# Gated mix of a long convolution and an MLP: the middle of the convolution in groups of four j

## The chip, the cores and the metric

The kernel runs on one core of one Trainium2 chip. Its engines are TensorE (PE, with its weight loads listed as PEld), VectorE (DVE), ScalarE (ACT), GpSimd (POOL) and SyncE (SP), which issues most DMA transfers. The metric is the time of one execution on the device, in microseconds, as the median of several runs; lower is better.

## What is computed

```python
def _A_ref(q, k, v, shift_k, ssm_k, ssm_D):
    ...
    for t in range(ks):
        k_shift = k_shift + k_pad[:, t:t + S, :] * shift_k[:, ks - 1 - t][None, None, :]
    kv = k_shift * v
    L = 2 * S
    kv_pad = jnp.pad(kv, ((0, 0), (0, S), (0, 0)))
    kf_pad = jnp.pad(ssm_k, ((0, 0), (0, S)))
    ...
    y_f = kv_f * kf_f[None, :, :, :]
    y = (lambda x, s, axes=(-2,-1): jnp.fft.irfft2(x, s=s, axes=axes))(y_f, (1, L), axes=(1, 2))[:, 0, :S, :]
    y = y + kv * ssm_D[None, None, :]
    return q * y

def _B_ref(x, w1, w2):
    h = jnp.einsum("bsd,df->bsf", x, w1)
    zero = jnp.zeros_like(h)
    h = jnp.maximum(h, zero)
    return jnp.einsum("bsf,fd->bsd", h, w2)

g = _sigmoid((x * gate_w).sum(-1, keepdims=True))
return g * a + (1 - g) * b
```

The sequence has S = 2048 positions and D = 512 channels; the hidden width of the MLP is 1792. `a` is a causal convolution of 2048 taps for each channel, done by a Fourier transform of length 4096, `b` is an MLP of two matrix products, and both are float32.

## The kernel before, in words

**The MLP** is cut into four chunks of 512 positions and 14 slices of 128 hidden units. `mlp1(c, f)` (lines 305 to 307) makes one slice of the hidden layer in a PSUM bank, with twelve matmuls of 128x128 weights and 512 columns: each float32 operand is split into a high and a low part, and three products stand for one. ACT (L317, `hh`) applies the maximum and DVE (L320, `hl`) makes the low part, after which the bank is free. `mlp2(c, f)` (L332 to L334) adds the slice to four output banks `m2`, again with twelve such matmuls. In this text they are called full matmuls.

**The convolution** is a transform in two stages, 64 by 32 points, as matrix products. In the first stage (`stage1`, L371) float32 matmuls with 64 rows and 128 columns turn two inputs, the filter ("h") and the product of the shifted k and v ("x"), into 64 complex frequencies; ACT copies each bank to `ev` (L376), and SP stores it to the DRAM array `sa`. A matmul that uses only a part of PE's 128x128 array is a *tile* here: tiles in different rows or columns of the array can run together. Two tiles of 64x128 fill the array once, and one filling is called a *round*.

In the middle (`conv_mid(j)`, L453 to L501, for 32 values of j) a load `r` brings both inputs of j; tiles of 64 rows and 32 columns (L476) apply the second stage, eight tiles for one j, into a bank `fh` for the filter and `fx` for the signal. Each bank holds real parts in its lower and imaginary parts in its upper 64 partitions. ACT copies the filter's halves (L486 to L488, so that both orders of real and imaginary are at hand), DVE forms the complex product (`y`, `hb`, `ha`: L491, L492, L494, L495), ACT and DVE split it into high and low (`yh` L496, `yl` L497), and three full matmuls with constants `ci` from POOL's queue apply the first inverse stage (`three`, L446 to L448). ACT copies the bank to `bv` (L500), and SP stores it to the DRAM array `sb`. At the end (`conv_end`, L551) two positions n at a time go through the last inverse stage with tiles of 128 rows and 64 columns (`y`), and DVE forms the gated output.

**Order.** The program is written out by a planner (`Plan`). Every operation has a rank, a supposed duration, the operations that it depends on, and the buffers that it takes and gives back; at each moment the planner lets each engine take the ready operation of lowest rank. Convolution work on PE has ranks that start with 0, MLP work ranks that start with 1, so that the MLP fills PE between the pieces of the convolution. `SAFE` is an extra margin before an operation counts as ready. The result is one fixed order for each engine, with semaphores between them.

**PSUM** has eight banks here: four `m2` outputs, and four `cv` banks that `mlp1`, `stage1`, the middle and the end share.

Of the kernel before, what the change touches and what calls it, by code (L numbers as in the profile page):

```python
# [39 lines left out]
def _constants():  # L40
# [5 lines left out]
    s1 = np.stack([s1, s1.reshape(P, NJ, 2, 2)[:, :, ::-1].reshape(P, P)], 1)  # L46


    fw = np.zeros((NJ, 2, 2, 32, 2, 2, 32))
    iv = np.zeros((NJ, 2, 2, 32, 32, 2, 2))  # L50
    n2, k2 = np.arange(32)[:, None], np.arange(32)[None]
    kc = np.arange(32)[:, None]
    for j in range(NJ):
        for b in range(2):
            k1 = 2 * j + b
            c = _w((4 * k1 + 1 + 256 * k2) * n2)
            fw[j, b, 0, :, 0, b] = c.real
            fw[j, b, 1, :, 0, b] = -c.imag
            fw[j, b, 0, :, 1, b] = c.imag
            fw[j, b, 1, :, 1, b] = c.real  # L60
            c = np.conj(_w((4 * k1 + 1 + 256 * kc) * n2.T))
            iv[j, 0, b, :, :, b, 0] = c.real
            iv[j, 1, b, :, :, b, 0] = -c.imag
            iv[j, 0, b, :, :, b, 1] = c.imag
            iv[j, 1, b, :, :, b, 1] = c.real

    cf = np.stack([fw[:, b, :, :, :, b] for b in range(2)], 1)
    cf = np.stack([cf, cf[:, ::-1]], -3).reshape(NJ, P, P).transpose(1, 0, 2)
    ih, il = _split(iv.reshape(NJ, P, P))
    ci = np.ascontiguousarray(np.stack([ih, il], 1).transpose(2, 0, 1, 3))  # L70
# [4 lines left out]
    return s1, cf, ci, ib  # L75
# [7 lines left out]
class Plan:  # L83
# [6 lines left out]
    def add(self, eng, dur, rank, fn, deps=(), take=(), give=(), dma=0, fifo=()):  # L90
        rank = tuple(_flat(rank))
        op = dict(eng=eng, dur=dur, rank=rank, fn=fn, take=tuple(take), give=tuple(give), dma=dma, fifo=tuple(fifo),
# [10 lines left out]
    def order(self):  # L103
# [4 lines left out]
        out = []  # L108
# [9 lines left out]
        while True:  # L118
            for eng, ops in ready.items():
                if busy.get(eng, 0.0) > now + 1e-9:  # L120
                    continue
                best = None
                for op in ops:
# [4 lines left out]
                    if any(self.turn[q][0] != op["n"] for q in op["fifo"]):  # L128
                        continue
# [27 lines left out]
            while events and events[0][0] <= now + 1e-9:  # L157
                _, _, what, op = heapq.heappop(events)
                if what == "go":
                    ready.setdefault(op["eng"], []).append(op)  # L160
                    continue
# [3 lines left out]
                for o in op["next"]:  # L165
# [4 lines left out]
                    if not o["wait"]:  # L170
# [19 lines left out]
MM = 0.227  # L190
# [5 lines left out]
def build(tc, wf, xp, qn, kn, vn, hn, dn, sh, gw, w1, w2, cs1, ccf, cci, cib, out):  # L196
# [12 lines left out]
    sb = dram.tile([32, P, D], F32, name="sb")  # L209
    bd = dram.tile([16, P, D], F32, name="bd")  # L210

    room = {"raw": RAW, "x": XB, "cv": 4, "hh": 2, "m20": 1, "m21": 1, "m22": 1, "m23": 1, "o": OB, "in": IN, 
            "cf": 2, "acc": ACC, "tmp": TMP, "ev": EV, "r": RB, "ci": CIB, "ha": HAB, "y": YB, "yh": YHB, "bv": BVB,
# [99 lines left out]
    def mlp1_out(c, f, prev):  # L313
        i = c * NF + f

        def relu():
            nc.scalar.activation(tile_of(("hh", c, f), "hh", dt=F32R, p=mp, bufs=2), T["m1", c, f], AF.Relu)  # L317

        def rest():
            nc.vector.scalar_tensor_tensor(tile_of(("hl", c, f), "hl", dt=F32R, p=mp, bufs=2), T["m1", c, f], 0.0,  # L320
# [5 lines left out]
    def mlp2(c, f):  # L326
        i = c * NF + f
        for s in range(4):
# [7 lines left out]
            m2[c, s] = add("PE", 3 * MM, (1, i + 1.5, s), go, [hdone[c, f], wdone[1, f], m2.get((c, s))],  # L336
# [28 lines left out]
    def stage1(t, c, key, rank, after, give):  # L365
        for r in range(R):
            def go(r=r):
                z = slice(r * D, (r + 1) * D)
                for half in range(2):
                    at = slice(64 * half, 64 * half + 64)  # L370
                    mm(bank(("s1" + t, c, half, r)), T["s1t",][at, P * "hx".index(t):P * "hx".index(t) + P], T[key][at, z], start=True, stop=True)  # L371

            m = add("PE", SWITCH + TILES, (0, rank), go, [after, s1ld], ["cv", "cv"], give if r == R - 1 else ())
# [69 lines left out]
    def three(key, h, l, i, z):  # L443
        ps = bank(key)
        c = T["ci", key[1]][:, 2 * P * i:2 * P * (i + 1)]
        mm(ps, c[:, :P], T[h][:, z], start=True, stop=False)  # L446
        mm(ps, c[:, :P], T[l][:, z], start=False, stop=False)  # L447
        mm(ps, c[:, P:], T[h][:, z], start=False, stop=True)  # L448
# [250 lines left out]
```

## Time and profile before

| what | value |
|---|---|
| median of 3 runs | 439.27 us (438.4 to 439.63) |
| the profiled execution | 439.54 us |
| its span, first to last instruction | 437.8 us |
| mean granted clock of TensorE | 0.997 |
| moved by DMA | 98.35 MB, mean 225 GB/s |

A page of the profile lists busy time by engine, the chain of work that ended last, and groups of equal instructions with the mean length of one and the idle time before them. Rows in order of time have start, length, engine, line, operation, output and inputs, shape of weights, shape of operands and count. A float32 matmul appears as two passes, so that 256 tiles of the middle stand as 512 rows. Since matmuls are pipelined, the length of one is more than the distance to the next.

### The profile page before, as it was taken

Reading aid. Unit: us, or ns where it says so; the run is one execution under the profiler, and the core shown is the slowest. Engines: PE = TensorE matmul, PEld = TensorE weight load, DVE = VectorE, ACT = ScalarE, POOL = GpSimd, SP = SyncE. Lnnn points to the kernel's source line nnn. Section 1 sums busy time; section 2 is a strip of 40 time slices with the busy share of each in tenths; the row PEclk is TensorE's granted clock in tenths of the full one; section 3 lists DMA queues with packets and bytes.
Section 4 is the critical chain, followed back from the end, with each engine's and each line's share of the span. In section 5 each row is a group of like instructions: output and inputs, shape, how many; then the busy total and the mean of one; then the engine's idle time right before and its main releaser. Section 6 shows DMA issues by size and latency. Waiting matters only on the chain.

```text
span 437.8 us, 6154 instructions
## 1 busy us (share of the span) xinstructions
PE 428.2 (98%) x2157; PEld 288.4 (66%) x2157; DVE 286.0 (65%) x426; ACT 195.0 (45%) x355; POOL 18.3 (4%) x38
## 2 busy tenths in 40 slices
PE   8999999999999999999999999999999999999994
PEld 6575665675856675665665565567877777758883
DVE  4699999869574119778887989878047654631113
ACT  4535445436344316767777778766123211101110
POOL 0000000000000010100100010100000000000000
PEclk9999999999999999999999999999999999999998
DMA  8988897897969395867689688731477888800002
GB/s 270 339 316 277 296 298 277 277 308 272 298 212 362 132 301 150 244 203 253 195 290 297 203 264 254 230 120 52 146 290 251 322 322 271 290 7 0 1 0 96
DMA packets 51616, 98.35 MB, mean 225 GB/s; under 512 B 5073, under 2 KB 9937, under 8 KB 51458
## 3 DMA queue, kind: packets, MB, share of 16 engines
q1 hardware_dynamic: 46898, 93.61, 63.4%
q0 software_dynamic: 4688, 4.36, 4.5%
q8 instruction: 17, 0.28, 0.3%
q14 instruction: 13, 0.11, 0.1%
HBM read 65.44 MB, written 32.51 MB: 224 GB/s over the span
## 4 chain that ended last, share of the span: by engine, by line
PE 92%; DVE 3%; DMA 2%; ACT 1%; issue 0%; DVEq 0%; SPq 0%; ACTq 0%
PE m L332 13%; PE m L305 12%; PE m L334 11%; PE m L333 11%; PE m L307 11%; PE m L306 11%; PE fh L476 6%; PE s1h L371 4%; PE s1x L371 4%; PE y L551 3%; PE iv L446 2%; PE iv L447 2%; PE iv L448 1%; DMA raw<-w 1%; DMA ev<-wf 1%; DVE hl L320 1%
## 5 line engine op out<-in xcount | busy, mean ns | idle before, releaser
L332 PE MATMUL m<-w1h_h,hh 128*128 128x512 f32 x224 | 91.2, 407 | 0.9 <-ACT hh L317 0.9
L320 DVE SCALAR_TENSOR_TENSOR hl<-m,hh 128x512 fp32r<-128x512 f32 x56 | 38.5, 689 | 76.8 <-ACT hh L317 76.5
L334 PE MATMUL m<-w1h_h,hl 128*128 128x512 f32 x224 | 87.6, 391 | 0.1
L333 PE MATMUL m<-w1l_l,hh 128*128 128x512 f32 x224 | 87.4, 390 | 0.0
L317 ACT ACTIVATE hh<-m 128x512 fp32r<-128x512 f32 x56 | 33.4, 598 | 118.3 <-PE m L307 113.8
L305 PE MATMUL m<-xh_h,w0h_h 128*128 128x512 f32 x192 | 77.8, 405 | 0.0
L307 PE MATMUL m<-xh_h,w0l_l 128*128 128x512 f32 x192 | 75.0, 391 | 0.0
L306 PE MATMUL m<-xl_l,w0h_h 128*128 128x512 f32 x192 | 74.9, 390 | 0.0
L332 PEld LDWEIGHTS m<-w1h_h,hh 128*128 128x128 f32 x224 | 42.0, 187 | 34.8 <-issue 25.5
L305 PEld LDWEIGHTS m<-xh_h,w0h_h 128*128 128x128 f32 x192 | 36.0, 187 | 26.6 <-issue 14.7
L334 PEld LDWEIGHTS m<-w1h_h,hl 128*128 128x128 f32 x224 | 42.0, 188 | 9.8 <-DVE hl L320 0.5
L333 PEld LDWEIGHTS m<-w1l_l,hh 128*128 128x128 f32 x224 | 42.1, 188 | 7.7
L307 PEld LDWEIGHTS m<-xh_h,w0l_l 128*128 128x128 f32 x192 | 36.0, 188 | 8.0
L306 PEld LDWEIGHTS m<-xl_l,w0h_h 128*128 128x128 f32 x192 | 36.1, 188 | 6.7
L476 PE MATMUL fx<-r,cf 64*32 64x512 f32 x256 | 34.0, 601 | 0.0
L476 PE MATMUL fh<-r,cf 64*32 64x512 f32 x256 | 33.8, 601 | 0.0
L491 DVE TENSOR_TENSOR y<-fx,ha 128x512 f32<-128x512 f32 x32 | 22.1, 690 | 12.5 <-ACT ha L487 11.2
L428 DVE TENSOR_TENSOR acc<-acc,tmp 128x1024 f32<-128x1024 f32 x24 | 29.3, 1222 | 0.6
L486 ACT COPY ha<-fh 64x512 f32<-64x512 f32 x32 | 18.5, 579 | 23.5 <-PE fx L476 13.6
L464 POOL DMA_DIRECT2D ci<-cci x32 | 16.9, 529 | 274.1 <-DMA sa<-ev 152.3
L497 DVE TENSOR_TENSOR yl<-ha,yh 128x512 fp32r<-128x512 f32 x32 | 22.0, 689 | 5.1 <-ACT yh L496 4.8
L376 ACT COPY ev<-s1x 128x512 f32<-128x512 f32 x32 | 17.1, 595 | 17.7 <-PE s1x L371 14.0
(67 smaller groups left out, 514.2 us busy)
## 6 DMA issues: line engine op xcount, KB each, us to landing
sa<-ev SPq DMA_DIRECT2D x64, 256.0 KB, 2.7
r<-sa SPq DMA_DIRECT2D x32, 512.0 KB, 4.6
sb<-bv SPq DMA_DIRECT2D x32, 256.0 KB, 3.3
br<-sb SPq DMA_DIRECT2D x16, 512.0 KB, 4.8
raw<-w SPq DMA_DIRECT2D x26, 256.0 KB, 4.6
in<-kn SPq DMA_DIRECT2D x10, 512.0 KB, 5.4
raw<-xp SPq DMA_DIRECT2D x16, 256.0 KB, 4.6
in<-hn SPq DMA_DIRECT2D x8, 512.0 KB, 5.5
```

The lines of the kernel that those rows point to most:

```text
L305: mm(ps, part("h", f, k), T["x", "h", c, k], start=k == 0, stop=False)
L306: mm(ps, part("h", f, k), T["x", "l", c, k], start=False, stop=False)
L307: mm(ps, part("l", f, k), T["x", "h", c, k], start=False, stop=k == 3)
L317: nc.scalar.activation(tile_of(("hh", c, f), "hh", dt=F32R, p=mp, bufs=2), T["m1", c, f], AF.Relu)
L320: nc.vector.scalar_tensor_tensor(tile_of(("hl", c, f), "hl", dt=F32R, p=mp, bufs=2), T["m1", c, f], 0.0, T["hh", c, f].bitcast(F32), op0=O ...
L332: mm(ps, T["hh", c, f][:, z], T["w", "h", 1, f], start=f == 0, stop=False)
L333: mm(ps, T["hh", c, f][:, z], T["w", "l", 1, f], start=False, stop=False)
L334: mm(ps, T["hl", c, f][:, z], T["w", "h", 1, f], start=False, stop=f == NF - 1)
L371: mm(bank(("s1" + t, c, half, r)), T["s1t",][at, P * "hx".index(t):P * "hx".index(t) + P], T[key][at, z], start=True, stop=True)
L428: nc.vector.tensor_tensor(T["acc", c], T["acc", c], T[dst], op=OP.add)
L476: mm(ps[to:to + 32, :], cf[at, co:co + 32], r[at, z], start=True, stop=True)
L491: y = add("DVE", d, rank, lambda: tt(tile_of(k("y"), "y"), T[k("fx")], T[k("ha")], op=OP.mult), [fx, q2], ["y"], fifo=["y"])
```

## The change

**First stage.** The two pairs of tiles of one call are now one operation that takes four banks and needs one entry into tiles, where two operations of two banks were ordered by themselves. The constant table is half as large.

**Middle.** `conv_mid(g)` does four j at a time, for eight g. The forward tiles keep their 64x32 shape, but each round now writes, for one of real (o = 0) or imaginary (o = 1), the four j of one parity b to a bank of its own: two rounds for the filter, each an operation by itself, two for the signal in one or two pieces as the planner puts them. Real and imaginary parts so lie on the same partitions of different banks. ACT and DVE copy the filter's four banks to `ha`; DVE multiplies the signal's banks with them (eight products) and adds in four steps to `p`, which stays in float32 and isn't split. The first inverse stage is then sixteen float32 tiles of 32 rows and 64 columns, one row strip for each j and one bank for each j, in two rounds that add up. ACT and DVE copy two banks each to `bv`. Loads of `r` are one for each j and input; the constants of forward and inverse come together in `cc` on SP's queue, and POOL's loads of `ci` are gone. `sb` has another layout.

**Planner.** An operation says whether it is in tiles, and entering tiles is charged only once for neighbours. While ready work of rank 1 needs no bank, other rank 1 work may not take banks that a waiting tile operation needs. `SAFE` for PE goes from 2.1 to 1.0, there are three buffers `hh` for two, and `mlp2` is ranked one slice later.

```diff
-        for r in range(R):
-            def go(r=r):
+        def go():
+            for r in range(R):
                 z = slice(r * D, (r + 1) * D)
...
-            m = add("PE", SWITCH + TILES, (0, rank), go, [after, s1ld], ["cv", "cv"], give if r == R - 1 else ())
+        m = add("PE", R * TILES, (0, rank), go, [after, s1ld], ["cv"] * 2 * R, give, tiles=True)
...
+        def rounds(t, os):
+            for o in os:
+                ps = [bank(k("f", t, o, b)) for b in range(2)]
+                for j in range(4):
+                    for b in range(2):
+                        at = slice(64 * b, 64 * b + 64)
+                        mm(ps[b][32 * j:32 * j + 32, :], T[k("cc")][at, 64 * j + 32 * o:64 * j + 32 * o + 32],
+                           T[k("r", t, j // 2)][at, (j % 2) * D:(j % 2 + 1) * D], start=True, stop=True)
...
+                    def mul(o=o, b=b, i=i):
+                        src = T[k("ha", i ^ o, b)]
+                        tt(src if o else tile_of(k("p", i, b), "p"), T[k("f", "x", o, b)], src, op=OP.mult)
...
+                        def join(b=b, i=i):
+                            tt(T[k("p", i, b)], T[k("p", i, b)], T[k("ha", 1 - i, b)], op=OP.add if i else OP.subtract)
...
-        iv = add("PE", 3 * MM, (0, rank), lambda: three(k("iv"), k("yh"), k("yl"), 0, first), [yl, ci], ["cv"], ["yh", "ci"])
+        def inverse():
+            ps = [bank(k("iv", j)) for j in range(4)]
+            for o in range(2):
+                for b in range(2):
+                    for j in range(4):
+                        at = slice(32 * j, 32 * j + 32)
+                        c = 2 * P + P * o + 64 * b
+                        mm(ps[j][64 * b:64 * b + 64, :], T[k("cc")][at, c:c + 64], T[k("p", o, b)][at, :], start=o == 0, stop=o == 1)
+
+        iv = add("PE", 2 * TILES, (0, rank), inverse, list(y.values()), ["cv"] * 4, ["p"] * 4 + ["cc"], tiles=True)
...
-sb[n::16].rearrange("h p d -> p h d")
+sb[:, n::16]
...
-SAFE = dict(PE0=2.1, PE1=0.175, ACT=0, DVE=0.4)
+SAFE = dict(PE0=1.0, PE1=0.175, ACT=0, DVE=0.4)
...
+HHB = 3
+M2R = 2.5
```

Three places show what moves. On PE, in the first stage of the convolution before (`s1x` is the signal's tiles, L332 to L334 one part of `mlp2`):

```order
L371 MATMUL s1x_0_0_529<-acc_375,s1c_s1t 128x512
L371 MATMUL s1x_1_0_531<-acc_375,s1c_s1t 128x512
L332 MATMUL m_0_1_210<-w1h_h_5_392,hh_5_459 128x512
...
L371 MATMUL s1x_0_1_546<-acc_375,s1c_s1t 128x512
L371 MATMUL s1x_1_1_548<-acc_375,s1c_s1t 128x512
```

and there now (`s1h` is the filter, L341 to L343 `mlp2`, L314 the next `mlp1`, which takes a bank):

```order
L380 MATMUL s1x_0_0_394<-acc_284,s1c_s1t 128x512
L380 MATMUL s1x_1_0_396<-acc_284,s1c_s1t 128x512
L380 MATMUL s1x_0_1_398<-acc_284,s1c_s1t 128x512
L380 MATMUL s1x_1_1_400<-acc_284,s1c_s1t 128x512
L341 MATMUL m_0_0_202<-w1h_h_4_266,hh_4_350 128x512
...
L343 MATMUL m_0_3_244<-w1h_h_4_266,hl_4_367 128x512
L380 MATMUL s1h_0_0_444<-in_343,s1c_s1t 128x512
L380 MATMUL s1h_1_0_446<-in_343,s1c_s1t 128x512
L380 MATMUL s1h_0_1_448<-in_343,s1c_s1t 128x512
L380 MATMUL s1h_1_1_450<-in_343,s1c_s1t 128x512
L314 MATMUL m_0_5_465<-xh_h_0_102,w0h_h_5_369 128x512
```

The four tiles of one call now stand together, with twelve full matmuls to the next four.

On PE, in the middle before (`fh` and `fx` are the forward tiles of one j, `iv` the inverse of an earlier j):

```order
L334 MATMUL m_1_3_1158<-w1h_h_9_673,hl_9_1668 128x512
L476 MATMUL fh_1798<-r_1613,cf_1473 32x512 x4
L476 MATMUL fx_1799<-r_1613,cf_1473 32x512 x4
L446 MATMUL iv_1809<-yh_1766,ci_1638 128x512
L447 MATMUL iv_1809<-yl_1777,ci_1638 128x512
L448 MATMUL iv_1809<-yh_1766,ci_1638 128x512
L305 MATMUL m_1_11_1821<-xh_h_0_976,w0h_h_11_800 128x512
```

and now (`iv_1` is the inverse of group 1 with a bank for each j, `f_x` the signal of group 2):

```order
L343 MATMUL m_1_3_1160<-w1h_h_12_790,hl_12_1855 128x512
L524 MATMUL iv_1_1899<-p_0_1_1763,cc_1534 64x512
L524 MATMUL iv_1_1900<-p_0_1_1763,cc_1534 64x512
L524 MATMUL iv_1_1901<-p_0_1_1763,cc_1534 64x512
L524 MATMUL iv_1_1902<-p_0_1_1763,cc_1534 64x512
...
L524 MATMUL iv_1_1902<-p_1_1_1784,cc_1534 64x512
L341 MATMUL m_1_0_1087<-w1h_h_13_912,hh_13_1874 128x512
...
L343 MATMUL m_1_1_1097<-w1h_h_13_912,hl_13_1890 128x512
L476 MATMUL f_x_0_2_1941<-r_x_2_1768,cc_1726 32x512
...
L476 MATMUL f_x_1_2_1956<-r_x_2_1781,cc_1726 32x512
```

The inverse is sixteen tiles in a block, six full matmuls stand behind it, and then both rounds of the next signal follow in one block.

On DVE, in the middle now, for one group (products L506, copies L493, sums L513, an MLP slice L329):

```order
L506 TENSOR_TENSOR p_0_3_2159<-f_x_0_3_2137,ha_0_3_2032 128x512
...
L506 TENSOR_TENSOR ha_1_3_2034<-f_x_1_3_2150,ha_1_3_2034 128x512
L493 COPY ha_0_4_2205<-f_h_0_4_2186 128x512
L513 TENSOR_TENSOR p_0_3_2159<-p_0_3_2159,ha_0_3_2058 128x512
L513 TENSOR_TENSOR p_0_3_2167<-p_0_3_2167,ha_0_3_2032 128x512
L513 TENSOR_TENSOR p_1_3_2172<-p_1_3_2172,ha_1_3_2060 128x512
L493 COPY ha_0_4_2232<-f_h_0_4_2209 128x512
L513 TENSOR_TENSOR p_1_3_2180<-p_1_3_2180,ha_1_3_2034 128x512
L329 SCALAR_TENSOR_TENSOR hl_3_2255<-m_2_3_2221,hh_3_2249 128x512
```

Copies of the next group's filter now stand on DVE among the sums that the inverse waits for; before, all of the filter's copies were on ACT.

More of the change, by code (lines that the diff above doesn't have):

```diff
@@ L56, in _constants @@
             c = _w((4 * k1 + 1 + 256 * k2) * n2)
[L57 to L70, printed above, removed]
+            fw[b, 0, :, j, 0] = c.real
+            fw[b, 1, :, j, 0] = -c.imag
+            fw[b, 0, :, j, 1] = c.imag
+            fw[b, 1, :, j, 1] = c.real
+            c = np.conj(c.T)
+            iv[j % 4, :, j // 4, 0, b, 0] = c.real
+            iv[j % 4, :, j // 4, 1, b, 0] = -c.imag
+            iv[j % 4, :, j // 4, 0, b, 1] = c.imag
+            iv[j % 4, :, j // 4, 1, b, 1] = c.real
+    cc = np.concatenate([fw.reshape(P, 8, 2 * P), iv.reshape(P, 8, 2 * P)], 2)
     c = np.conj(_w((4 * np.arange(64)[:, None] + 1) * 32 * np.arange(64)[None])) / S
     ib = np.stack([c.real, -c.imag], 1).reshape(P, 64)
-    return s1, cf, ci, ib
+    return s1, cc, ib
 def _flat(r):
@@ L88, in __init__, with add @@
         self.room, self.ops, self.turn = dict(room), [], {}
[L90 removed]
+    def add(self, eng, dur, rank, fn, deps=(), take=(), give=(), dma=0, fifo=(), tiles=False):
         rank = tuple(_flat(rank))
[L92 removed]
+        op = dict(tiles=tiles, eng=eng, dur=dur, rank=rank, fn=fn, take=tuple(take), give=tuple(give), dma=dma, fifo=tuple(fifo),
                   wait=0, next=[], n=len(self.ops))
@@ L107, in order @@
         pipe = 0.0
-        out = []
+        out, soon, mode = [], [], False
         for op in self.ops:
@@ L122, in order @@
                 best = None
+                held = ()
+                if eng == "PE" and any(o["rank"][0] == 1 and not o["take"] for o in ops):
+                    held = {t for o in ops + soon if o["rank"][0] == 0 and len(o["take"]) > 1 for t in o["take"]}
                 for op in ops:
@@ L128, in order @@
                     if any(self.turn[q][0] != op["n"] for q in op["fifo"]):
+                        continue
+                    if op["rank"][0] and any(t in held for t in op["take"]):
                         continue
@@ L143, in order @@
                 free = now + op["dur"]
+                if eng == "PE":
+                    if op["tiles"] and not mode:
+                        free += SWITCH
+                    mode = op["tiles"]
                 if eng == "PE" and now < PE_COLD:
@@ L193, with build @@
 ROW = P * D * 4
-def build(tc, wf, xp, qn, kn, vn, hn, dn, sh, gw, w1, w2, cs1, ccf, cci, cib, out):
+def build(tc, wf, xp, qn, kn, vn, hn, dn, sh, gw, w1, w2, cs1, ccc, cib, out):
     nc = tc.nc
@@ L370, in go @@
                     at = slice(64 * half, 64 * half + 64)
-                    mm(bank(("s1" + t, c, half, r)), T["s1t",][at, P * "hx".index(t):P * "hx".index(t) + P], T[key][at, z], start=True, stop=True)
-            m = add("PE", SWITCH + TILES, (0, rank), go, [after, s1ld], ["cv", "cv"], give if r == R - 1 else ())
+                    mm(bank(("s1" + t, c, half, r)), T["s1t",][at, :], T[key][at, z], start=True, stop=True)
+        m = add("PE", R * TILES, (0, rank), go, [after, s1ld], ["cv"] * 2 * R, give, tiles=True)
+        for r in range(R):
             for half in range(2):
@@ L605, in build @@
     p2 = add("SP", 0.0, -1e3, lambda: phase(2), stores)
-    for j in range(NJ):
-        conv_mid(j, p2)
+    for g in range(NJ // 4):
+        conv_mid(g, p2)
     p3 = add("SP", 0.0, -1e3, lambda: phase(3), sbstores)
@@ L646 @@
 RB = 4
-CIB = 4
-HAB = 2
-YB = 1
-YHB = 2
-BVB = 2
+HS = 1
+XS = 1
+HD = 1
+VD = 1
+HHB = 3
+M2R = 2.5
+HAB = 8
+PB = 4
+BVB = 4
 BRB = 4
```

128 lines of the change are left out of this document (65 added, 63 removed).

## The prediction

> **What bounds the kernel now.** I read the page's busy shares first, then the chain that ended last, then PE's own waits, then PE's rows in order of time.
>
> ```profile
> PE 428.2 (98%) x2157; PEld 288.4 (66%) x2157; DVE 286.0 (65%) x426; ACT 195.0 (45%) x355; POOL 18.3 (4%) x38
> PE 92%; DVE 3%; DMA 2%; ACT 1%; issue 0%; DVEq 0%; SPq 0%; ACTq 0%
> 160.00:300.00 140.00, 139.09 (x948) 84.94 (x947) 116.24 (x173) 100.33 (x176) 14.78 (x28) 1.00 0.72 222
> PE iv L446 <- DVE hl L320: 0.9, 1, 0.9
> ```
>
> The first two rows are totals and chain: PE is busy 98% of the span and is 92% of the chain. The third is the stretch from 160 to 300 us, where the middle of the convolution runs between MLP matmuls (columns: length, busy PE, PEld, DVE, ACT, POOL, clock, DMA share, GB/s): PE is full at clock 1.00, DVE 83%, ACT 72%. The fourth is the only wait of PE in that stretch, 0.9 us. So the time is PE's work added up, and each piece counts by the distance between starts, not by its own length, since neighbours overlap. Four prices are needed.
>
> ```profile
> 427.18 0.39 PE L332 MATMUL m<-w1h_h,hh 128*128 128x512 f32 x1
> ...
> 431.71 0.39 PE L334 MATMUL m<-w1h_h,hl 128*128 128x512 f32 x1
> ```
>
> **Full matmul**: 20 steps in 4.53 us, 0.227 us each.
>
> ```profile
> 229.70 0.39 PE L334 MATMUL m<-w1h_h,hl 128*128 128x512 f32 x1
> 230.02 0.63 PE L476 MATMUL fh<-r,cf 64*32 64x512 f32 x4
> 230.04 0.63 PE L476 MATMUL fx<-r,cf 64*32 64x512 f32 x4
> 230.47 0.61 PE L476 MATMUL fh<-r,cf 64*32 64x512 f32 x4
> 230.50 0.61 PE L476 MATMUL fx<-r,cf 64*32 64x512 f32 x4
> 231.04 0.50 PE L446 MATMUL iv<-yh,ci 128*128 128x512 f32 x1
> 231.37 0.39 PE L447 MATMUL iv<-yl,ci 128*128 128x512 f32 x1
> ```
>
> **Round of tiles**: eight float32 tiles of 64x32 start within hundredths of a microsecond of each other and run side by side, in two passes, 230.02 and 230.47. The next round could start 0.43 later again, so a round is 2 x 0.43 = 0.86 us. **Entry**: from 229.70 to 231.37 are 1.67 us, in which two full matmuls start (0.45): the block costs 1.22, thus 0.86 of work and 0.36 for going into and out of tiles.
>
> ```profile
> 124.00 0.39 PE L334 MATMUL m<-w1h_h,hl 128*128 128x512 f32 x1
> 124.32 1.99 PE L371 MATMUL s1x<-acc,s1c_s1t 64*128 64x512 f32 x8
> 126.24 0.50 PE L332 MATMUL m<-w1h_h,hh 128*128 128x512 f32 x1
> 126.57 0.40 PE L333 MATMUL m<-w1l_l,hh 128*128 128x512 f32 x1
> 126.81 0.39 PE L334 MATMUL m<-w1h_h,hl 128*128 128x512 f32 x1
> 127.13 1.99 PE L371 MATMUL s1h<-in,s1c_s1t 64*128 64x512 f32 x8
> 129.05 0.50 PE L305 MATMUL m<-xh_h,w0h_h 128*128 128x512 f32 x1
> 129.38 0.40 PE L306 MATMUL m<-xl_l,w0h_h 128*128 128x512 f32 x1
> ```
>
> Two first-stage pairs back to back: 124.00 to 126.57 is 2.57, less 0.45 is 2.12, so an entry here is 2.12 - 1.72 = 0.40 and a pair alone would cost 1.26. Columns of 64 stand between the two:
>
> ```profile
> 325.57 0.39 PE L307 MATMUL m<-xh_h,w0l_l 128*128 128x512 f32 x1
> 325.89 1.94 PE L551 MATMUL y<-br,ibt_ibt 128*64 128x512 f32 x8
> 327.75 0.50 PE L305 MATMUL m<-xh_h,w0h_h 128*128 128x512 f32 x1
> 328.09 0.40 PE L306 MATMUL m<-xl_l,w0h_h 128*128 128x512 f32 x1
> ```
>
> Two rounds of tiles with 64 columns cost 2.52 - 0.45 = 2.07: again 0.86 a round, 0.35 the entry. A round costs the same as two tiles of 64 rows, two of 64 columns, or eight of 64x32.
>
> **The change, part by part.** Entries are counted in the order of PE's instructions.
>
> ```profile
> L446 PE MATMUL iv<-yh,ci 128*128 128x512 f32 x32 | 13.4, 419 | 0.9 <-DVE hl L320 0.9
> L447 PE MATMUL iv<-yl,ci 128*128 128x512 f32 x32 | 12.5, 390 | 0.0
> L448 PE MATMUL iv<-yh,ci 128*128 128x512 f32 x32 | 12.6, 392 | 0.0
> ```
>
> *Inverse stage.* Out go 96 full matmuls (three groups of 32), 96 x 0.227 = 21.8 us. In come eight blocks of sixteen 32x64 tiles, two rounds each. No row shows a tile of 32 rows. From below a round is 0.86: a pass streams 512 columns whatever the tile's shape, and all three shapes above take 0.43 a pass. From above it is 1.72, if only half of the eight tiles ran at a time. I take 0.86, the value of all three shapes; the row with 64 columns is nearest, so 2.07 a block: 8 x 2.07 = 16.6. **-5.2 us**.
>
> *Forward stage.* 256 tiles before and after, eight to a round: 32 rounds, no change of work. Before, 30 rounds stand alone and two together, 31 entries; now the filter's rounds stand alone (16) and the signal's in twos (8), 24 entries. 7 x 0.36: **-2.5 us**.
>
> *First stage.* 32 rounds both times; 26 entries before (20 alone, 6 doubles), 16 doubles now. 10 x 0.40: **-4.0 us**.
>
> *Waits that go.* The 0.9 us at 272 belongs to an inverse group that waited on DVE behind a chain through ACT and back (sum, copy, subtract). The copy and the subtraction are gone. **-0.9 us**.
>
> *Waits that come.* All four banks that PE, ACT and DVE share are now taken at once, by each first-stage group and by each inverse. First stage: the rows above show what that costs. s1x fills four banks at 124.32, only three full matmuls (0.7 us) follow, s1h fills the four again, and the step from 126.81 to 127.13 (0.32) is the same as that from 124.00 to 124.32: nothing waited. In the new order groups come in pairs with twelve matmuls (2.7 us) between the two, seven times, and an MLP matmul that needs a bank often follows the second directly. Lower end 0, upper end a bank's copy each time:
>
> ```profile
> L376 ACT COPY ev<-s1h 128x512 f32<-128x512 f32 x32 | 17.3, 592 | 15.3 <-PE s1h L371 11.8 <-DMA sa<-ev 3.1 <-ACT ev L376 0.4
> L495 DVE TENSOR_TENSOR ha<-y,hb 128x512 f32<-128x512 f32 x32 | 22.1, 691 | 1.0
> L320 DVE SCALAR_TENSOR_TENSOR hl<-m,hh 128x512 fp32r<-128x512 f32 x56 | 38.5, 689 | 76.8 <-ACT hh L317 76.5
> ```
>
> 16 x 0.59 = 9.4. At 129.05 an MLP matmul also followed a group of four with no wait, so I stay near 0: **+1.0 us**, for two or three full waits where ACT has an MLP tile ahead of the copies.
>
> *Middle, other engines.* A group of four j had 4 x 5 DVE instructions; now it has 8 products, 4 sums, 2 copies of ha and 2 of bv, 16 at about 0.69 = 11.0 us where there were 13.8. ACT goes from five copies per j to four per group. What must be in time is the chain from f_x to its inverse: 8 products, 4 sums, the next group's 2 copies, and up to 2 hl, 16 x 0.69 = 11.0 us. PE has there 42 full matmuls (9.5), two lone forward rounds (2.4) and f_x itself (2.1): 14.0. The chain hides with 3 us to spare, so 0; without that cover, it costs what it is late, eight times.
>
> *Loads.* 32 constant loads on POOL's queue go (128 KB each, 4.2 of 98 MB); SP issues 64 loads of r with 256 KB for 32 of 512 KB, and br reads rows that lie apart.
>
> ```profile
> br<-sb SPq DMA_DIRECT2D x16, 512.0 KB, 4.8
> in<-hn SPq DMA_DIRECT2D x8, 512.0 KB, 5.5
> ```
>
> hn is read in rows that lie apart, 5.5 us against 4.8. br has four buffers, two blocks of y ahead (some 18 us), which hides 0.7; without that, 8 x 0.7 = 5.6. I take 0, and 0 for the smaller loads.
>
> **Sum**, against the profiled execution's own 439.54 us: -5.2 - 2.5 - 4.0 - 0.9 + 1.0 = -11.6, so 427.9. That execution lies 0.3 above the median of the runs (439.27), within their spread; I say **428.0**.
>
> **A rule weighed.** In the y block the loads of weights show:
>
> ```profile
> 325.88 0.20 PEld L551 LDWEIGHTS y<-br,ibt_ibt 128*64 128x64 f32 x4 [0.35 <-issue]
> 326.37 0.14 PEld L551 LDWEIGHTS y<-br,ibt_ibt 128*64 128x64 f32 x2 [0.29 <-issue]
> ```
>
> Weights of 0.14 us load at 326.37 while tiles over the same 128 rows run, and the block's two rounds still cost 0.86 each. The Trainium skill, page "TensorE: Matmul & The Clock Gate", section "The mechanism" of its part on packing small matmuls, says that weight loads overlap running matmuls only where the row group differs. By that, the inverse, whose second round uses each tile again, would show its loads; the trace does not agree for y.
>
> **Rivals.**
> 1. *Weights show in the inverse.* As mechanism: three of a block's four passes wait 0.14 for weights, 8 x 3 x 0.14 = +3.4: **431.3**. For it: tiles of 32 rows are unseen. Against: the y rows just shown.
> 2. *Four banks at once are a new wait.* After an inverse, six matmuls (1.4 us) stand before f_x, which needs two of its banks; a copy takes 0.6 to 0.7 after the matmul's end, and a DVE instruction ahead of it 0.69 more. If that happens in all eight groups (5.5) and half of the first-stage groups wait a copy (4.7, less the 1.0 already counted): +9.2, **437**; half of that is **432.5**, which I take as its likely size. For it: DVE and ACT stand at 83% and 72% before, and the Trainium skill, page "TensorEngine Tiling (Array Packing)", section "PSUM Bottleneck", warns that emptying the banks becomes the limit once tiles make the matmuls faster. Against: 126.81 to 127.13, and fewer instructions on both engines.
> 3. *The 32x64 tiles don't all run side by side* (slower than before). If four of the eight run at a time, a round is 1.72: 8 x 1.72 = +13.8, **441.8**. It decides from a round of 0.86 + 11.6/16 = 1.58 on. For it: no row has four row strips. Against: three shapes, one price.
> 4. *The tiles of a block are not adjacent in time* (the change doesn't do what it says): a tile block split by a late bank pays its entry again, 24 x 0.36 = +8.6 at most, **436.6**.
>
> **How the numbers follow.** Forecast 428.0 with 426 to 430: 0.66. Rival 1: 0.06. Rival 2: 0.16, from 430 to 437. Rival 3: 0.07, from 437 up to 442. Rival 4: 0.05. Low end: besides, a hitch of the old order may go, seen in two rows of the chain (start, length):
>
> ```profile
> 21.26 1.47 PE s1h L371 x4
> ...
> 38.74 1.06 PE s1h L371 x4
> ```
>
> The same work is 0.4 longer at 21 us. Without it, without the 1.0 added, and with the 0.9 by which the fastest run before lay under the median: 425.6. High end: rival 2 up to three quarters of its price and rival 1, 435. About 0.86 lie within. A measurement of this kernel can't tell less than about 0.3% (1.3 us) from no change. Faster by more than that holds in the forecast, rivals 1 and 4, and nearly all of rival 2: 0.92; within 0.3%: 0.03, the low end of rival 3 and the last of rival 2; slower: 0.05, the rest of rival 3.
>
> **What would show it.** PE's rows: blocks of sixteen iv tiles at 2.07 us between full matmuls (2.5 is rival 1, 3.8 rival 3); f_x at 2.07, lone f_h at 1.22, stage-one groups at 2.12; 56 entries. PE's waits: not over 1 us each after s1h and none in front of iv or f_x (rival 2 has them there, put down to copies on ACT or DVE). If PE's blocks hold these prices and the time still isn't 428, the sum has missed a wait at the start or the end.

## The result, and the profile after

The changed kernel takes **426.31 us** (median of 4 runs, 425.87 to 426.52) against 439.1 for the kernel before on the same chip: a ratio of 0.9708, 95% interval 0.9692 to 0.9725, or 12.8 us less. The profiled execution took 426.14 with a span of 424.4, which is 13.4 less than the span before. The forecast was 428.0 in a range of 425.6 to 435.0.

The page of the changed kernel, in the order read before: busy shares, then the engines' shares of the chain that ended last.

```profile
PE 416.2 (98%) x2317; PEld 277.5 (65%) x2317; DVE 256.4 (60%) x394; ACT 120.3 (28%) x227; POOL 1.4 (0%) x6
PE 96%; DMA 2%; DVE 1%; issue 1%; ACT 0%; DVEq 0%; ACTq 0%
```

PE still bounds the kernel: it lost 12.0 us of busy time and is 96% of the chain instead of 92%. ACT lost 75 us and DVE 30, which is worth nothing by itself, since neither set the end. The stretch in which the middle runs now (columns: length, then busy PE, PEld, DVE, ACT, POOL, clock, DMA share, GB/s):

```profile
160.00:320.00 160.00, 160.00 (x1238) 96.90 (x1237) 98.47 (x157) 36.47 (x65) 0.34 (x1) 1.00 0.53 178
```

PE is never idle there, at clock 1.00; DVE is at 62% (it was 83%) and ACT at 23% (it was 72%). All of PE's waits in the whole execution (total, times, longest):

```profile
PE warm L610 <- DVE zero_zero L605: 1.2, 1, 1.2
PE m L341 <- ACT hh L326: 0.9, 1, 0.9
PE m L314 <- ACT ev L386: 0.2, 1, 0.2
```

The first two belong to the start and were there before (the second varies between 0.9 and 2.2 us in the executions below, so up to about 1 us of any difference can be that). The wait of `iv` on `hl`, 0.9 before, is gone, and one of 0.2 behind a first-stage group is new. A wait of 0.8 in the start (L289 on `gh_h`) is gone too, but the start gained only 0.1 by all its differences: the first `mlp1` matmul on PE that uses `w0h_h` stands at 14.28 us, before at 15.75 with six full matmuls (1.36 us) more ahead of it. PE's rows in a steady group of the middle:

```profile
263.58 0.39 PE L343 MATMUL m<-w1h_h,hl 128*128 128x512 f32 x1
263.89 1.97 PE L524 MATMUL iv<-p,cc 32*64 32x512 f32 x32
265.80 0.50 PE L341 MATMUL m<-w1h_h,hh 128*128 128x512 f32 x1
266.13 0.39 PE L342 MATMUL m<-w1l_l,hh 128*128 128x512 f32 x1
...
267.06 0.40 PE L343 MATMUL m<-w1h_h,hl 128*128 128x512 f32 x1
267.39 1.95 PE L476 MATMUL f_x<-r_x,cc 64*32 64x512 f32 x32
269.26 0.50 PE L341 MATMUL m<-w1h_h,hh 128*128 128x512 f32 x1
269.60 0.39 PE L342 MATMUL m<-w1l_l,hh 128*128 128x512 f32 x1
```

From 263.58 to 266.13 are 2.55 us, in which two full matmuls start: the block of sixteen 32x64 tiles costs 2.55 - 0.45 = **2.10**. The signal's block beside it costs 2.54 - 0.45 = 2.09. The new tiles have the price of the old ones.

Measured in this way at each of PE's blocks, the difference is:

| part | before, us | after, us | difference | forecast |
|---|---|---|---|---|
| inverse stage | 96 x 0.227 = 21.8 | 8 x 2.10 = 16.8 | -5.0 | -5.2 |
| forward stage, with the `iv` wait | 39.9 | 36.2 | -3.7 | -2.5 - 0.9 |
| first stage, with its waits | 38.5 | 34.3 | -4.2 | -4.0 + 1.0 |
| last stage (`y`) | 16.6 | 16.6 | 0 | 0 |
| sum | | | -12.9 | -11.6 |

The span differs by 13.4; 0.1 of the other 0.5 lies in the start, the rest in steps of a tenth or two between full matmuls that have no name.

### The profile page after: what moved, and what is told of

It is laid out like the page before. It is cut to its first block, busy times and chain, and to the rows that moved or that the text cites. A ratio compares the mean times of both kernels' runs of the same rounds, so it can differ in the third digit from the quotient of the medians.

```text
span 424.4 us, 6184 instructions
## 1 busy us (share of the span) xinstructions
PE 416.2 (98%) x2317; PEld 277.5 (65%) x2317; DVE 256.4 (60%) x394; ACT 120.3 (28%) x227; POOL 1.4 (0%) x6
## 4 chain that ended last, share of the span: by engine, by line
PE 96%; DMA 2%; DVE 1%; issue 1%; ACT 0%; DVEq 0%; ACTq 0%
PE m L341 13%; PE m L314 12%; PE m L343 12%; PE m L315 12%; PE m L316 12%; PE m L342 12%; PE f_h L476 4%; PE iv L524 4%; PE f_x L476 4%; PE y L586 4%; PE s1h L380 3%; PE s1x L380 3%; PE m L298 2%; DMA sa<-ev 1%; PE warm L610 1%
## 5 line engine op out<-in xcount | busy, mean ns | idle before, releaser
L341 PE MATMUL m<-w1h_h,hh 128*128 128x512 f32 x224 | 92.0, 411 | 0.9 <-ACT hh L326 0.9
L343 PE MATMUL m<-w1h_h,hl 128*128 128x512 f32 x224 | 87.6, 391 | 0.1
L329 DVE SCALAR_TENSOR_TENSOR hl<-m,hh 128x512 fp32r<-128x512 f32 x56 | 38.5, 689 | 81.4 <-ACT hh L326 81.2
L314 PE MATMUL m<-xh_h,w0h_h 128*128 128x512 f32 x192 | 76.6, 399 | 0.2 <-ACT ev L386 0.2
L341 PEld LDWEIGHTS m<-w1h_h,hh 128*128 128x128 f32 x224 | 42.0, 187 | 40.2 <-issue 28.9
L314 PEld LDWEIGHTS m<-xh_h,w0h_h 128*128 128x128 f32 x192 | 36.0, 188 | 19.9 <-issue 10.8
L343 PEld LDWEIGHTS m<-w1h_h,hl 128*128 128x128 f32 x224 | 42.1, 188 | 10.1 <-DVE hl L329 1.0
L506 DVE TENSOR_TENSOR p<-f_x,ha 128x512 f32<-128x512 f32 x32 | 19.9, 682 | 10.9 <-PE f_x L476 10.9
L535 DVE COPY bv<-iv 128x512 f32<-128x512 f32 x16 | 10.3, 686 | 21.8 <-PE iv L524 21.8
L386 ACT COPY ev<-s1x 128x512 f32<-128x512 f32 x32 | 16.8, 599 | 18.2 <-PE s1x L380 10.0
L386 ACT COPY ev<-s1h 128x512 f32<-128x512 f32 x32 | 16.8, 598 | 15.8 <-PE s1h L380 13.4
L435 DVE TENSOR_TENSOR tmp<-in,sht_sht 128x512 f32<-128x512 f32 x32 | 21.3, 682 | 0.0
L513 DVE TENSOR_TENSOR p<-p,ha 128x512 f32<-128x512 f32 x32 | 20.7, 681 | 0.0
L506 DVE TENSOR_TENSOR ha<-f_x,ha 128x512 f32<-128x512 f32 x32 | 19.8, 678 | 0.0
```

What stands on the lines that cost most here:

```text
L314: mm(ps, part("h", f, k), T["x", "h", c, k], start=k == 0, stop=False)
L341: mm(ps, T["hh", c, f][:, z], T["w", "h", 1, f], start=f == 0, stop=False)
L343: mm(ps, T["hl", c, f][:, z], T["w", "h", 1, f], start=False, stop=f == NF - 1)
L386: nc.scalar.copy(tile_of(("ev" + t, c, half, r), "ev"), T["s1" + t, c, half, r])
L506: tt(src if o else tile_of(k("p", i, b), "p"), T[k("f", "x", o, b)], src, op=OP.mult)
```

## The experiments

Each was timed beside the kernel before on its chip (439.1 to 439.45). Diffs are against the changed kernel, except for the two in which the first stage alone is changed.

**What a round of the new tiles costs.** The inverse block is issued twice, so that its outcome is written a second time:

```diff
-            for o in range(2):
-                for b in range(2):
-                    for j in range(4):
+            for o, b, j in [(o, b, j) for _ in range(2) for o in range(2) for b in range(2) for j in range(4)]:
+                if True:
+                    if True:
```

> The changed kernel with each inverse block issued twice (32 tiles in four rounds instead of 16 in two; the second pair writes the same values again). Theory (the time is PE's work added up, and a round of eight 32x64 tiles costs 0.86 us inside a block): 8 blocks x 2 rounds x 0.86 = +13.8 us on 426.3, so 440.1. Rival (the gain came from DVE, ACT and DMA, and PE has slack in the middle): well under that, 426 to 431.

439.99 us, ratio 1.0015 (0.9999 to 1.0032). PE's rows of this run:

```profile
270.10 0.39 PE L343 MATMUL m<-w1h_h,hl 128*128 128x512 f32 x1
270.41 3.69 PE L524 MATMUL iv<-p,cc 32*64 32x512 f32 x64
...
274.37 0.39 PE L342 MATMUL m<-w1l_l,hh 128*128 128x512 f32 x1
```

A block of four rounds costs 4.27 - 0.45 = 3.82, so two more rounds are 1.72 and one is 0.86, with nothing for weights. Had a round been 1.72, as the third rival had it, the whole change would have stood about here, at no gain.

**Does the order inside the block matter?** Here both products of one tile follow each other, where the kernel has eight tiles between them:

```diff
-            for o in range(2):
-                for b in range(2):
-                    for j in range(4):
+            for b in range(2):
+                for j in range(4):
+                    for o in range(2):
```

> The changed kernel with the two products of one tile issued directly after each other (o innermost) instead of eight different tiles and then the same eight again. Theory A (PE starts tiles strictly in program order, so that a tile's second product holds back the next tile): blocks become chains of eight tiles, each 0.86 us later than the one ahead, some 7.7 us instead of 1.7, +6.0 x 8 = +48 us, about 474. Theory B (each tile has a queue of its own and the order within a block doesn't matter): 426.3. Anything between says that a few instructions can be passed.

426.61 us, ratio 0.9715 (0.97 to 0.9729): no difference that these runs can tell.

PE's rows, and the passes that run just after the start (columns as in the windows of PE alone: length, busy, clock, DMA share, GB/s):

```profile
263.96 0.39 PE L343 MATMUL m<-w1h_h,hl 128*128 128x512 f32 x1
264.28 2.02 PE L524 MATMUL iv<-p,cc 32*64 32x512 f32 x32
...
266.57 0.39 PE L342 MATMUL m<-w1l_l,hh 128*128 128x512 f32 x1
```

```profile
264.35:264.75 0.40, 0.40 (x8) 1.00 0.79 276
```

The block costs 2.61 - 0.45 = 2.16, or 0.06 more than in the changed kernel. All eight tiles are running by 264.35 (eight passes run side by side there, as in a round of the changed kernel, and the next eight start 0.4 us later), although in the program each is followed by a second product on itself: what waits for its part of the array is passed by tiles behind it.

**How much slack has the chain to the inverse?** Dummy additions (four, then eight) are put on DVE ahead of the last sum of each group:

```diff
                         def join(b=b, i=i):
+                            if i and b:
+                                for _ in range(4):
+                                    tt(..."junk"..., T[k("p", i, b)], T[k("ha", 1 - i, b)], op=OP.add)
```

> The changed kernel with four more DVE additions of 128x512 per group, ahead of the last sum that the inverse waits for (results unused): 4 x 0.68 = 2.7 us more on DVE per group, 22 us in all. Theory (the chain from f_x to the inverse is hidden by 2.7 to 6.9 us of slack, which is what lies between the end of the last sum and the start of the inverse in the profile of the changed kernel): within 0.5 us of 426.3. Rival (the time was gained by a lighter DVE): up to +22, 448; half of it 437.

> As the run before with eight additions, 5.4 us more per group. Theory (slack of 2.7, 6.4, 6.2, 6.9, 4.0, 4.0, 4.0, 4.9 us in the eight groups): waits of 2.9 + 0 + 0 + 0 + 1.6 x 3 + 0.7 = +8.4 us, about 435, all of them in front of the inverse. Rival (DVE's sum counts): +44, 470.

With four: 428.71 us, ratio 0.9763 (0.9747 to 0.978), 2.4 more than the changed kernel. The eight inverse blocks cost 2.92, 2.12, 2.10, 2.10, 2.25, 2.25, 2.25 and 3.13, which is 2.3 over 8 x 2.10. At most 0.5 was expected: most of the 22 us that were added on DVE is hidden, but the slack is smaller than the expectation had it. With eight: 453.77, ratio 1.0331 (1.0304 to 1.0358), 27.5 more and three times what was expected. PE's waits in that run:

```profile
PE iv L527 <- DVE ha L493: 6.8, 4, 2.7
PE m L343 <- DVE hl L329: 4.2, 3, 2.9
PE iv L527 <- DVE hl L329: 1.8, 2, 1.3
```

The inverse waits for DVE's copy `ha`, not for the sum. The rows of one such place, PE and DVE:

```profile
275.11 1.07 PE L527 MATMUL iv<-p,cc 32*64 32x512 f32 x4
276.23 0.69 DVE L516 TENSOR_TENSOR p<-p,ha 128x512 f32<-128x512 f32 x1
276.83 0.69 DVE L493 COPY ha<-f_h 128x512 f32<-128x512 f32 x1
277.57 1.50 PE L527 MATMUL iv<-p,cc 32*64 32x512 f32 x10 [1.39 <-DVE ha L493]
```

Two tiles (four passes) of the fifth block start at 275.11. The last sum ends at 276.92, but the third tile and all behind it start only at 277.57, when the copy of the next group's filter has ended (277.52). That copy frees one of the four banks that the inverse takes. In the changed kernel's own rows, DVE and, for PE, the block quoted above:

```profile
259.21 0.68 DVE L513 TENSOR_TENSOR p<-p,ha 128x512 f32<-128x512 f32 x1
260.46 0.69 DVE L493 COPY ha<-f_h 128x512 f32<-128x512 f32 x1 [0.57 <-PE f_h L476]
```

the sum ends at 259.89, the copy at 261.15, and the inverse starts at 263.89: the chain's slack is 2.74, set by the copy. Some pieces then add up. An addition delays what follows by 0.73 (two last 1.42 and one 0.69): four are 2.92, 0.18 over the slack, and three of the blocks lost 0.15; eight are 5.8, 3.1 over it, and two of the blocks lost 3.05 (5.15 for 2.10). The seventh block is the other of these two. The sixth waits the same 1.39 us and still lost 4.2, since the granted clock was halved there; in the first block it was halved too (columns as in the window from 160 to 320):

```profile
190.70:194.00 3.30, 2.99 (x26) 0.85 (x26) 0.25 (x1) 0.00 (x0) 0.00 (x0) 0.50 0.00 0
299.90:303.20 3.30, 3.30 (x22) 1.40 (x10) 1.29 (x2) 1.08 (x2) 0.00 (x0) 0.50 0.11 32
```

In the sixth, 5.67 us lie between the end of the wait and the next `f_x` (298.27 to 303.94), where the fifth has 4.08 (277.57 to 281.65): 1.6 us for the clock. The first block lost 5.2, 2.65 of it as one wait, and the last 3.9; MLP matmuls behind the late `hl` waited 4.2. The eight blocks together are 20.9 of the 27.5.

**A late bank in front of the signal's tiles.** Three DVE instructions are put ahead of the copy of the inverse's first bank:

```diff
+                def late(j=j):
+                    for _ in range(3 if j == 0 else 0):
+                        tt(..."junk"..., T[k("iv", j)], T[k("cc")][:, :D], op=OP.add)
+                    nc.vector.tensor_copy(tile_of(k("bv", j), "bv"), T[k("iv", j)])
```

> The changed kernel with three more DVE operations of about 0.69 us ahead of the copy of each inverse's first bank, so that this bank comes free 2.1 us later. In the profile of the changed kernel that copy ends 0.77 us ahead of f_x, which takes the bank. Theory (four banks at once are hidden by that 0.77 us, less about 0.2 for the signal): f_x waits about 2.1 - 0.6 = 1.5 us in seven of eight groups, +10.5, about 437. Rival (PE has other slack there): 426 to 429.

433.47 us, ratio 0.9875 (0.9852 to 0.9897): 7.2 more, for 10.5 expected. PE's rows at one such block, with DVE's copies of the inverse's banks:

```profile
271.17 0.40 PE L343 MATMUL m<-w1h_h,hl 128*128 128x512 f32 x1
271.50 1.09 PE L476 MATMUL f_x<-r_x,cc 64*32 64x512 f32 x16
272.10 1.28 DVE L538 COPY bv<-iv 128x512 f32<-128x512 f32 x2
272.83 1.68 PE L476 MATMUL f_x<-r_x,cc 64*32 64x512 f32 x16 [0.24 <-DVE bv L538]
```

and the passes of those tiles in three stretches (length, busy PE with the passes that run in it, clock, DMA share, GB/s):

```profile
271.50:271.90 0.40, 0.40 (x8) 1.00 0.00 0
272.85:273.25 0.40, 0.40 (x1) 1.00 0.12 20
273.45:273.85 0.40, 0.40 (x8) 1.00 1.24 282
```

The mechanism is the second rival's, and it is there, in seven groups. Its size is another. The first round starts at 271.50 with all eight tiles: its two banks are not those that DVE copies. The first tile of the second round starts at 272.83, when DVE's first copy has ended (272.79), and runs alone; the other seven start near 273.40, when the second copy has ended (273.38). (The eighth pass of the third stretch is the second one of the tile that ran alone.) A second round would have started at 271.50 + 0.86 = 272.36, so the block is 1.05 late; seven blocks cost 3.15 instead of 2.09, 7 x 1.07 = 7.5. The expectation had the seven groups right, but had put the delay in front of the whole block, against a slack of 0.77. The list of waits shows less than a quarter of the loss:

```profile
PE f_x L476 <- DVE bv L538: 1.7, 7, 0.2
```

0.24 for each block is all that PE is idle; one tile that runs alone for 0.6 us counts as busy. In the changed kernel DVE's copies end at 267.22 and ACT's at 267.08:

```profile
265.93 1.29 DVE L535 COPY bv<-iv 128x512 f32<-128x512 f32 x2 [2.64 <-PE iv L524]
266.01 1.07 ACT L533 COPY bv<-iv 128x512 f32<-128x512 f32 x2 [3.45 <-PE iv L524]
```

The block starts at 267.39 and its second round 0.86 later, at 268.25: ACT's banks have 0.3 us to spare, DVE's 1.03. Here DVE's copies came 2.06 later (272.10 for 270.04, where the first addition starts), and 2.06 - 1.03 is the 1.05.

**The first stage apart.** Its two pairs are ordered singly again, the rest stays (21 blocks of first-stage tiles for 16):

```diff
-        def go():
-            for r in range(R):
+        for r in range(R):
+            def go(r=r):
...
-        m = add("PE", R * TILES, (0, rank), go, [after, s1ld], ["cv"] * 2 * R, give, tiles=True)
-        for r in range(R):
+            m = add("PE", TILES, (0, rank), go, [after, s1ld], ["cv", "cv"], give if r == R - 1 else (), tiles=True)
```

> The changed kernel with the first stage planned in operations of two banks again: 21 entries into tiles there instead of 16 (some pairs stay together by themselves). Theory (an entry costs 0.40 us, all else hides): +2.0 us, 428.3. Rival (groups of four banks bring waits that separate pairs don't have): the same or faster than 426.3.

428.69 us, ratio 0.9761 (0.9743 to 0.9778): 2.4 more, where five entries of 0.40 made 2.0. Counted in PE's rows, its first-stage blocks cost 36.8 us for 34.3, that is 2.5. Its wait at the start is longer (1.9 for 0.9), which puts the first `w0h_h` matmul 0.5 later (14.79 for 14.28); steps elsewhere give that back.

**The first stage alone.** The kernel before with the new planner and grouped first stage, but its old middle:

```diff
+                if eng == "PE":
+                    if op["tiles"] and not mode:
+                        free += SWITCH
+                    mode = op["tiles"]
...
-        m = add("PE", SWITCH + TILES, (0, rank), go, [after, s1ld], ["cv", "cv"], give if r == R - 1 else ())
+        m = add("PE", R * TILES, (0, rank), go, [after, s1ld], ["cv"] * 2 * R, give, tiles=True)
...
-SAFE = dict(PE0=2.1, PE1=0.175, ACT=0, DVE=0.4)
+SAFE = dict(PE0=1.0, PE1=0.175, ACT=0, DVE=0.4)
...
+HHB = 3
+M2R = 2.5
```

> The kernel before with the planner, the margin of 1.0, the three hh buffers and the first stage of the change, but with the old middle: 16 entries in the first stage for 26, 32 in the middle for 31, 8 at the end. Theory (entries alone): -10 x 0.40 + 0.36 = -3.6 us on 439.1, 435.5; what is left of the change's 12.8 us, about 9.2, is then the new middle. Rival (the new middle brought nearly all, the first stage nothing because waits for four banks eat it): 438 to 440.

439.38 us, ratio 1.0003 (0.9992 to 1.0014): no gain. The first stage did fall, from 38.5 to 34.0 us, but PE's waits and a place in the middle show where it went:

```profile
PE m L318 <- DVE hb L508: 2.7, 3, 1.3
```

```profile
270.04 0.69 DVE L508 TENSOR_TENSOR hb<-fx,hb 64x512 f32<-64x512 f32 x1
270.87 0.47 PE L318 MATMUL m<-xh_h,w0h_h 128*128 128x512 f32 x1 [0.69 <-DVE hb L508]
```

An MLP slice behind an inverse needs the bank `fx`, and DVE still reads that at the end of its long chain. The forward blocks cost 0.4 more, and other short waits on DVE and ACT make about 0.5; the rest of the 4.5 is not placed. The same with the margin of before left at 2.1 (the end of the diff against before, the rest as above):

```diff
 SAFE = dict(PE0=2.1, PE1=0.175, ACT=0, DVE=0.4)
...
+HHB = 3
+M2R = 2.5
```

> As s1_alone (first stage of the change with the old middle, 439.4), but with the old margin of 2.1 us ahead of a convolution operation on PE. In s1_alone some 4.5 us of waits came up in the old middle. Theory (the margin of 1.0 was too small for the old middle's chain through ACT and DVE, so that the first stage's gain was given back there): waits in the middle under 2 us, 435.5 to 437.5. Rival (the rule that holds banks back, or the third hh buffer, changes the old middle's order for the worse): about 439 again.

446.38 us, ratio 1.0153 (1.0124 to 1.0181), where 435.5 to 437.5 was expected. A longer margin made it worse, with a wait of 3.0 us behind a first-stage group and, in the middle, three kinds of shorter ones that add up to 2.2, 1.7 and 1.5 us. The granted clock was 0.50 for some 3.4 us twice, from 14.2 us and from 58.5 on, the second time behind the wait of 3.0. Its fastest execution, at a mean clock of 0.999, still took 444.31 us, so most of the loss is there without that.

**The margin in the changed kernel.**

```diff
-SAFE = dict(PE0=1.0, PE1=0.175, ACT=0, DVE=0.4)
+SAFE = dict(PE0=2.1, PE1=0.175, ACT=0, DVE=0.4)
```

> The changed kernel with the old margin of 2.1 us. PE has 55 entries into tiles instead of 56. Theory (the new middle has slack enough that the margin doesn't matter): 426.0 to 426.5. Rival (the margin moves groups of four banks to places where an MLP matmul needs a bank): 2 to 4 us more, with waits of PE m for ACT ev in the first stage.

431.28 us, ratio 0.981 (0.9788 to 0.9831): 5.0 more, with one block of tiles fewer (55). PE's rows and ACT's at the place of its longest wait:

```profile
52.43 1.99 PE L380 MATMUL s1x<-acc,s1c_s1t 64*128 64x512 f32 x8
57.01 2.50 ACT L386 COPY ev<-s1x 128x512 f32<-128x512 f32 x4 [3.50 <-DMA sa<-ev]
57.65 0.76 PE L314 MATMUL m<-xh_h,w0h_h 128*128 128x512 f32 x1 [3.23 <-ACT ev L386]
...
61.17 0.39 PE L316 MATMUL m<-xh_h,w0l_l 128*128 128x512 f32 x1
```

All four banks are full, ACT can't empty them because its `ev` buffers are still being stored, and an MLP slice that needs a bank stands next in PE's order. After 3.23 us of idle the granted clock is halved, which the windows show (columns as before):

```profile
58.00:61.00 3.00, 3.00 (x8) 2.35 (x8) 2.70 (x4) 1.41 (x3) 0.00 (x0) 0.50 0.55 199
```

From 57.65 to 61.17 are eight steps in 3.52 us, 1.7 more than 8 x 0.227. With 0.7 behind the products `p` and an entry less: 3.2 + 1.7 + 0.7 - 0.4 = 5.2. These rows belong to the profiled execution, which took 429.89 us, only 3.8 more than that of the changed kernel: some 1.4 came back in shorter steps in the start, in the first stage and at the end. That the median is 5.0 more lies in the other three executions, 431.09 to 431.70 us at a mean clock of 0.990 to 0.992 for 0.994. 0.004 of 430 us is 1.7, as much as one more such stretch at half clock would cost; no profile shows where it was.

**The loads taken out, put back.** The 32 constant loads of 128 KB are issued again on POOL's queue, and nothing reads them:

```diff
+        for u in range(4):
+            add("POOL", 1.04, (2, rank, u), lambda u=u: nc.gpsimd.dma_start(tile_of(k("ci", u), "ci", 2 * P, F32R, bufs=2), cci[:, 4 * g + u]), [cc])
```

> The changed kernel with 32 loads of 128 KB of constants back on POOL's queue (4.2 MB, read by nothing). Theory (PE's sum sets the time): within 0.5 us of 426.3. Rival (lighter DMA traffic is a part of the gain): slower by 1 us or more.

426.89 us, ratio 0.971 (0.9687 to 0.9734): 0.6 more, and the intervals overlap. POOL's busy time is back at 18.4 us and costs nothing that these runs can tell. The 0.6 goes with the granted clock: two executions took 426.05 and 426.25 us at a mean clock of 0.999 and 0.997, the other two 427.57 and 427.53 at 0.994 and 0.993. The profile is of one of these, and it shows a stretch at half clock in the start (columns as before):

```profile
14.60:17.90 3.30, 3.30 (x9) 2.60 (x8) 1.51 (x3) 0.08 (x1) 0.00 (x0) 0.50 0.84 319
```

Executions of other kernels, the one before among them, have such a mean clock now and then; whether the loads make it more frequent, four executions can't tell.

**Fewer blocks still.** Once by joining the filter's two rounds, once by taking four positions at a time in the last stage, with more buffers:

```diff
-HS = 1
+HS = 2
```

> The changed kernel with both rounds of the filter as one operation (four banks at once): 52 entries instead of 56, so by the entries alone 4 x 0.36 = -1.4 us, 424.9. Against it: the filter's block then takes all four banks, and the MLP's next slice waits until one is copied; three such waits of 0.8 us would make it 427.

427.09 us, ratio 0.972 (0.9703 to 0.9737): 52 blocks instead of 56 (eight fewer for the filter, but four of the signal's fell apart into single rounds), and no gain. Its waits:

```profile
PE m L314 <- DVE p L506: 1.4, 2, 0.7
PE m L314 <- ACT bv L533: 0.8, 1, 0.8
```

Three waits of about 0.7 behind a bank take what four entries gave.

```diff
-        if n % 2 == 0:
+        if n not in (3, 7, 11, 13, 15):
...
+        us = range(n - (3 if n < 12 else 1), n + 1)
...
-            for u in (n - 1, n):
+            for u in us:
...
-TB = 5
+TB = 6
...
-BRB = 4
+BRB = 6
```

> The changed kernel with the last inverse stage in groups of four positions where loads allow (0 to 3, 4 to 7, 8 to 11, then 12 and 13, 14 and 15; in the order of PE these last four stand together): 52 entries instead of 56, 4 x 0.35 = -1.4 us, 424.9. Against it: a group waits for four loads of 512 KB where six buffers hold one and a half groups; if the loads come late, PE waits or the last outputs come after the MLP's end, 427 or more.

**424.85 us** (424.41 to 424.87, 5 runs), ratio 0.9667 (0.965 to 0.9683): 1.5 less than the changed kernel, and the best of all. PE's row of a block of four:

```profile
347.12 0.39 PE L343 MATMUL m<-w1h_h,hl 128*128 128x512 f32 x1
347.44 3.65 PE L587 MATMUL y<-br,ibt_ibt 128*64 128x512 f32 x16
...
351.36 0.40 PE L342 MATMUL m<-w1l_l,hh 128*128 128x512 f32 x1
```

4.24 - 0.45 = 3.79 for what took two blocks of 2.07, and no new wait over 0.2 us.

## Why the prediction was right

**The bound** held: PE's blocks, counted by the distance between starts, explain 12.9 of the span's 13.4 us.

**Inverse stage**: the choice of 0.86 a round was right (2.10 measured for a block, 2.07 taken), and the doubled block shows the 0.86 by itself. This term, the largest, was the one that could have turned the sign.

**Forward stage**: -3.7 for -3.4 with the wait. The seven entries came; the rest is one old double that had cost 2.3 and not 2.1, which the sum had not looked at.

**First stage**: -4.2 for -3.0. The ten entries came; the added waits were mis-sized, about 0.4 where 1.0 was taken (for "two or three full waits", though two or three copies of 0.59 are 1.2 to 1.8), and the old order had about 0.6 of hitches in front of its groups that went. The one wait that shows is this:

```profile
54.35 1.99 PE L380 MATMUL s1h<-in,s1c_s1t 64*128 64x512 f32 x8
56.57 0.50 PE L314 MATMUL m<-xh_h,w0h_h 128*128 128x512 f32 x1 [0.23 <-ACT ev L386]
```

With the 0.4 that have no name, these make up the 1.8 us by which the profiled executions differ more than the sum.

**Other engines at 0**: right, with 2.74 us of slack in the steady groups for the 3 that were worked out. The term rested on the wrong link, though: the copy of the next filter bank closes the chain and not the sum, and the eight additions cost three times what was expected, since the slack was smaller, MLP matmuls waited as well and the granted clock was halved twice.

**Loads at 0**: right as far as tested; with 32 of them put back, the two executions without a halved clock took 426.05 and 426.25 us. The rows of `br` that lie apart (5.3 us to landing for 4.8) and the 64 smaller loads of `r` were not tried by themselves; no wait of PE in the changed kernel is put down to a load.

**Rivals.** The first (weights show) is refuted by 2.10 for a block while the weights' loads took 0.13 each:

```profile
L524 PEld LDWEIGHTS iv<-p,cc x256: 127/132/132, 187.3 to 317.9; 32*64 32x64 f32 x128
```

The third is refuted by the doubled block. The fourth: the blocks stayed whole, 56 entries as counted. The second did not come, but it was the one to fear: it is 0.3 us away in front of `f_x` on ACT's side and 1.03 on DVE's, it took most of what the first stage gained with the old middle, and with a margin of 2.1 it took 5.0 us. What kept it away in the first stage was the planner's shorter margin, which the prediction had not given any price.

**What each part is worth.** With the first stage planned apart, the kernel is faster than the one before by 10.4 us of 12.8. Of these, 1.7 are still the first stage, whose blocks cost 36.8 for 38.5 there (21 entries for 26); the new middle is the other 8.7, as in the table (5.0 + 3.7). Grouping the rest of the first stage brings 2.4 on top of it, and with the old middle the whole grouping brings nothing: there the MLP waits for banks that the middle still holds. The third `hh` buffer, the later rank of `mlp2` and the rule that holds banks back were not taken out one by one.

## What to carry to other kernels

Where PE is full, count its work by the distance between starts and its entries into tiles by the program's order: each entry saved gave 0.35 to 0.40 us wherever no bank came late. Before grouping, look for the last reader of each bank that the group takes, also a reader that belongs to the next group, and compare its end with the group's start. A planner's margin is a price to be tried out with every new order, since more of it cost 5.0 us in one middle and 7.0 in the other, halved clock included. And look at the granted clock of each execution before a difference of one or two microseconds is explained: one stretch of 3.4 us at half clock is up to 1.7.

## What the runs showed of the hardware

- Sixteen tiles of 32x64 in four row strips and two columns run eight at a time at 0.86 us a round of float32, the same as tiles of 64x32, 64x128 and 128x64.
- The order of tiles in a block costs next to nothing: 2.16 us with the products of a tile side by side, 2.10 with eight tiles between them.
- A tile that waits for a bank holds back all that stand behind it: with DVE's first copy ended at 272.79, the tile that needed it ran alone until 273.40, though three of the seven others write the same bank. A tile that waits only for its part of the array is passed by others. And the loss barely shows as idle time, 0.24 us of wait for 1.07 us lost.
- The granted clock of PE fell to 0.50 for some 3.4 us in or behind waits of quite different length: 3.23 us (`margin21`), 3.0 (`s1_alone_m2`), 2.65 and 1.39 (`chain8`), and in the start of `loads_back` behind waits of 1.9 and 0.2. Such a stretch with PE at work all through cost 1.6 to 1.7 us. The length of a wait does not decide alone: one of 2.90 us in `chain8` (209.2 to 212.1) left the clock at 1.00, so did one of 2.2 in the start of `chain4`, and of three waits of 1.39 in `chain8` only one was followed by it. No wait of 0.7 to 0.8 us in these runs was. The Trainium skill, page "TensorE: Matmul & The Clock Gate", section "What's actually happening", puts the halving after an idle window of about 3.4 us; all waits here were shorter than that, so by these traces a single wait need not be that long.
